# Retention and two MLPs on one core: free PSUM banks for two early steps, weight conversion one unit later, separate partial results for two stages

## The chip, the cores and the metric

The kernel runs on one core of a Trainium2 chip. The metric is the device time of one execution, in microseconds. Three runs of the kernel before are shown, with a median of 576.7 us (576.01 to 577.94).

## What is computed

Inputs are float32 q, k, v of shape 2 x 8 heads x 768 positions x 64, and a decay `lam` per head. The reference runs a chunked retention. For each head and each block of positions:

```python
intra = einsum('bhic,bhjc->bhij', qb, kb) * Dmask      # Dmask[i,j] = lam**(i-j), i >= j
intra = einsum('bhij,bhjd->bhid', intra, vb)
inter = einsum('bhid,bhde->bhie', qb * lam_pow, kv_state)
out   = intra + inter
kv_state = lam_block * kv_state + einsum('bhsd,bhse->bhde', kb * rev_pow, vb)
```

The result is reshaped to 1536 tokens x 512 and goes through two MLPs with float64 weights (512 x 2048 and 2048 x 512): `relu(x @ w_in)**2 @ w_out`, then `leaky_relu(x @ w_in, 0.01) @ w_out`.

## The kernel before, in words

**Retention** (function `retention`, lines 184 to 409) works on 12 units of 128 positions with all 8 heads: two batches of six. For a unit, SyncE (SP) loads k, q and v; TensorE transposes k and q (L294), ScalarE (ACT) copies the two transposes to SBUF (L298), VectorE (DVE) multiplies the transposed q by powers of `lam` straight out of PSUM (`scale_q`, L304); TensorE makes the scores (L311), DVE masks them with a table of powers (`mask`, L316), GpSimd (POOL) multiplies k by powers (L329), TensorE makes the state product (`state`, L335), DVE adds it to the state (L347, L349), and TensorE makes the output (`output`, L360 and L362), which ACT and DVE split into a high and a low part (L68, L69).

PSUM is one pool of eight banks (`bank()`, L58). A new bank is the one that has come free, so its first matmul waits for the last reader of what was in it. One bank, `idle`, is taken at the start for transposes that only keep TensorE at work (`warm`, L218).

The order on SP and TensorE is the order of the program text, written out by hand: for the first units in L368 to L390, then by the loop from L391, where pass i transposes unit i+2, loads units i+4 and i+2, makes state and output of unit i, masks unit i+1 and makes scores of unit i+2. On DVE, ACT and POOL the framework sets the order from its own reckoning of when operands are ready, except where `keep_in_program_order` puts an instruction behind the one traced before it on its engine.

**Weights** are float64 and are converted to float32 high and low parts on ACT and DVE from 1 MB raw tiles (`converting`, L98 to L144). A conversion is an ACT absolute value (L114) and seven DVE steps: L115, L116, L118, L121, L122, L125 and L137. `convert()` does the next step of what is at work. In the retention loop it is called once a pass for i = 3 to 9, with `pin=True`, which pins the DVE step that it yields and not the ACT operations. The raw tile itself is fetched in passes 1 and 9 (L398). In the MLPs `convert()` is called between groups of matmuls, without a pin.

**The first MLP** runs in four stages (l = 0, s = 0 to 3) of 512 hidden features. Stages 1 and 2 (`seven`) make the second product by seven multiplications instead of eight (`second_pair`, L617). Results go to DRAM tiles `spill`: `keep` (L607) copies a PSUM bank to one of nine SBUF buffers `f` (L61) and either stores it (SP) or adds it to what is there (an accumulating DMA issued by POOL, L613). Three products per pair, P1, P6 and P67, go to DRAM tiles `partial`: stage 1 stores them, stage 2 adds to them, and then ten DRAM-to-DRAM accumulating DMAs (L684) spread them over `spill`. In these two stages `activate_for_seven` (L479) holds eight of the nine `f` buffers in `later` until the sums of them are made.

Of the kernel before, what the change touches and what calls it, by code (L numbers as in the profile page):

```python
# [9 lines left out]
F32 = mybir.dt.float32  # L10
# [4 lines left out]
ALU = mybir.AluOpType  # L15
P = 128
# [3 lines left out]
def tile_retention_then_two_mlps(  # L20
# [12 lines left out]
    nc = tc.nc  # L33
    B, H, S, D = q.shape
# [4 lines left out]
    NP = H // 2  # L39
    TT = 512  # L40
# [9 lines left out]
    dram = ctx.enter_context(tc.tile_pool(name="dram", bufs=1, space=bass.MemoryType.DRAM))  # L50
# [7 lines left out]
    def bank():  # L58
        return psum.tile([P, 512], F32, tag="ps", name="ps")
# [113 lines left out]
    seven = {(0, 1), (0, 2)}  # L173
# [10 lines left out]
    def retention(ctx_att, att):  # L184
# [6 lines left out]
        tiny = ctx_att.enter_context(tc.tile_pool(name="tiny", bufs=1))  # L191

        units = [(b, c) for b in range(B) for c in range(NCH)]
        nats, qT, kT, qS, Pm, raw_scores = {}, {}, {}, {}, {}, {}

        def load(i, which="kqv"):
            b, c = units[i]
# [77 lines left out]
                DTr[:, par], bass.AP(tensor=row.tensor, offset=row.offset, ap=[[1, P], [2 * W, NP], [1, C]])))  # L275

        def column_of_powers():
            ps = bank()[:, 0:H]
            nc.tensor.transpose(ps, pw[:, 1:C + 1], ident[0:H, 0:H])
            nc.scalar.copy(kdec, ps)  # L280

# [6 lines left out]
        def transposes(i, names="kq"):  # L288
            for name in names:
                dst = {"k": kT, "q": qT}[name]  # L290
                ps = bank().rearrange("p (a s) -> p a s", a=NP)
                src = nats[i, name]
                for p in range(NP):
                    nc.tensor.transpose(ps[:, p, :], src[:, 2 * p:2 * p + 2, :].rearrange("s h d -> s (h d)"), ident)  # L294
                if i == 0:
                    warm(3 if name == "k" else 4)
                dst[i] = tr.tile([P, NP, C], F32, tag=name, name=name + "T", bufs=2)
                nc.scalar.copy(dst[i], ps)  # L298
            return ps

        def scale_q(i, ps):
            if units[i][1]:
                qS[i] = tr.tile([P, NP, C], F32, tag="qS", name="qS")
                ve.tensor_tensor(out=qS[i], in0=ps, in1=LR, op=ALU.mult)  # L304
# [8 lines left out]
        def mask(i):  # L313
            Pm[i] = wk.tile([P, 2, NP, C], F32, tag="Pm", name="Pm")
            for par in range(2):
                ve.tensor_tensor(out=Pm[i][:, par], in0=raw_scores[i][par], in1=DT[:, par], op=ALU.mult)  # L316
# [6 lines left out]
        def state(n):  # L323
            b, c = units[n]
            if c == NCH - 1:
                return
            kn, vn = nats[n, "k"], nats[n, "v"]
            kd = wk.tile([P, NP, 2, D], F32, tag="kd", name="kd")
            nc.gpsimd.tensor_tensor(  # L329
                out=kd, in0=kn.rearrange("s (a r) d -> s a r d", r=2),  # L330
                in1=kdec.rearrange("s (a r o) -> s a r o", r=2, o=1).to_broadcast([P, NP, 2, D]), op=ALU.mult)
            ps = bank()[:, 0:NP * D].rearrange("p (a e) -> p a e", a=NP)
            for p in range(NP):
                for par in range(2):
                    nc.tensor.matmul(ps[par * D:(par + 1) * D, p, :], kd[:, p, par, :], vn[:, 2 * p + par, :],  # L335
                                     start=True, stop=True)
            old, new = st[c % 2], st[(c + 1) % 2]
            if c:
                tmp = wk.tile([P, NP, D], F32, tag="tmp", name="tmp")
                for par in range(2):  # L340
                    r = slice(par * D, (par + 1) * D)
                    nc.gpsimd.tensor_tensor(out=tmp[r], in0=old[r, :, r],
                                            in1=LR[r, :, C - 1:C].to_broadcast([D, NP, D]), op=ALU.mult)
            for par in range(2):
                r = slice(par * D, (par + 1) * D)
                if c:
                    nc.vector.tensor_tensor(out=new[r, :, r], in0=ps[r], in1=tmp[r], op=ALU.add)  # L347
                else:
                    nc.vector.tensor_copy(new[r, :, r], ps[r])  # L349
# [32 lines left out]
        scale_q(1, q1)  # L382
        scores(1)
        state(0)
        mask(0)
        output(0)
        scale_q(2, transposes(2))
        state(1)
        mask(1)
        scores(2)  # L390
        for i in range(n_units):  # L391
            if i and i + 2 < n_units:
                scale_q(i + 2, transposes(i + 2))
            if i + 4 < n_units:
                load(i + 4, "kq")
            if i + 2 < n_units:
                load(i + 2, "v")
            if i in (1, 9):  # L398
                fetch()
            if i:  # L400
                if i > 1:
                    state(i)
                output(i)
                if i + 1 < n_units:
                    mask(i + 1)
                if i + 2 < n_units:
                    scores(i + 2)
            if 3 <= i <= 9:
                convert(pin=True)


# [190 lines left out]
            put(h, r22[h], r22[h], 1, 1)  # L602
            put(h, s2[h], s2[h], 0, 1)

    partial = [{n: dram.tile([P, TT], F32, name=f"partial{p}{n}") for n in ("P1", "P6", "P67")} for p in range(2)]

    def keep(src, dst, first):  # L607
        f = plain()
        nc.scalar.copy(f, src)  # L609
        if first:  # L610
            dma(dst, f)
        else:
            nc.gpsimd.dma_start(dst, f, accum_op=ALU.add)  # L613
# [1 line left out]


    def second_pair(s):  # L617
        begun = (0, s - 1) in seven
        (g0h, g0l), (g1h, g1l) = g[0], g[1]
        x = {  # L620
            "B11": [(g0h[:, 2 * h], g0l[:, 2 * h]) for h in range(2)],
            "B21": [(g0h[:, 2 * h + 1], g0l[:, 2 * h + 1]) for h in range(2)],
            "B22": [(g1h[:, 2 * h + 1], g1l[:, 2 * h + 1]) for h in range(2)],
            "T1": [(g1h[:, 2 * h], g1l[:, 2 * h]) for h in range(2)],
            "T2": [(tt[2][:, 0, h], tt[2][:, 1, h]) for h in range(2)],
        }
        ps = {}

        def product(p, where, a, b, start=True):
            if start:  # L630
                ps[p, where] = bank()
            ops = []
            for h in range(2):
                if a[0] == "A":
                    i, j = int(a[1]) - 1, int(a[2]) - 1
                    hi, lo = (w[:, j, (2 * p + i) * P:(2 * p + i + 1) * P] for w in wts[0, s, 1, h])
                else:
                    hi, lo = (sums[0, s, 1, h][:, part, int(a[1]) - 1, p] for part in range(2))
                bh, bl = x[b][h]
                ops += [(hi, bh), (hi, bl), (lo, bh)]  # L640
            three(ps[p, where], ops, start, True, not start)
            return ps[p, where]

        def kept(p, i, k):
            return spill[0][k][2 * p + i]

        def late_split(n, old, m):
            x[n] = x[old]
            with tc.high_priority(offset=400):
                for h in range(2):  # L650
                    split(*x[n][h], later[m(h)])

        both = range(2)
        for p in both:
            keep(product(p, "A", "A11", "B11"), partial[p]["P1"], not begun)
            yield True
        for p in both:
            keep(product(p, "C", "S1", "T1"), kept(p, 1, 1), False)
            yield True
        late_split("T3", "T1", lambda h: (1, 2 * h))  # L660
        for p in both:
            keep(product(p, "A", "A12", "B21", False), kept(p, 0, 0), False)
            yield True
        late_split("T4", "B21", lambda h: (0, 2 * h + 1))
        for p in both:
            keep(product(p, "C", "S4", "B22", False), kept(p, 0, 1), False)
            yield True
        for p in both:
            keep(product(p, "B", "S2", "T2"), partial[p]["P6"], not begun)
            yield True  # L670
        for p in both:
            keep(product(p, "D", "A22", "T4"), kept(p, 1, 0), False)
            yield True
        yield from first(0, s, 2)
        for p in both:
            keep(product(p, "B", "S3", "T3", False), partial[p]["P67"], not begun)
            yield True
        opened.add(("sums", 0, s + 1))
        if (0, s + 1) not in seven:
            for p in both:  # L680
                p1, p6, p67 = (partial[p][n] for n in ("P1", "P6", "P67"))
                for dst, src in ((p67, p1), (kept(p, 0, 1), p1), (kept(p, 0, 1), p6), (kept(p, 1, 0), p67),
                                 (kept(p, 1, 1), p67)):
                    nc.gpsimd.dma_start(dst, src, accum_op=ALU.add, max_dma_last_dim=TT)  # L684

    def second(l, s, t, ms=range(4)):
        last = s == NS - 1
# [94 lines left out]
```

## Time and profile before

| what | value |
|---|---|
| runs, median (lowest to highest) | 576.7 us (576.01 to 577.94) |
| the profiled execution's own time | 576.42 us |
| its span | 574.5 us |
| TensorE busy | 564.2 us, 98% |
| DVE busy | 418.4 us, 73% |
| ACT busy | 305.0 us, 53% |
| POOL busy | 83.9 us, 15% |
| granted TensorE clock | 1.0 of full speed in every slice |

The span lies inside the execution's own time, 1.92 us shorter. Busy shares are averages over stages with different limits, so a stage is read by the waits that end last there. L12 is line 12 of the kernel, and `ps` is any PSUM bank.

### The profile page before, as it was taken

How to read it: one execution, taken by the hardware profiler on the slowest of the kernel's cores; microseconds unless marked ns; L12 is line 12 of the kernel's file. 1: busy time of each engine (PE TensorE's matmuls, PEld its weight loads, DVE VectorE, ACT ScalarE, POOL GpSimd, SP SyncE). 2: the span in 40 equal slices, each digit the busy share in tenths (PEclk: the TensorE clock that was granted, in tenths of full speed). 3: DMA queues.
4: the chain of work that ended last, by engine and by line, in shares of the span. 5: the costliest groups of instructions: out<-in, count | busy, mean ns of one | idle time of the engine just before them, and what ended most of it. 6: DMA issues, size and time to landing. Idle time of an engine off the chain costs nothing.

```text
span 574.5 us, 8051 instructions
## 1 busy us (share of the span) xinstructions
PE 564.2 (98%) x3075; PEld 470.7 (82%) x3075; DVE 418.4 (73%) x589; ACT 305.0 (53%) x477; POOL 83.9 (15%) x101
## 2 busy tenths in 40 slices
PE   7989999999999999999999999999999999999997
PEld 6878888888788888888888888888888888888886
DVE  3879999999927599498478999929873996217222
ACT  2344598546757687758448374553562376225110
POOL 3426000000040105445000000000203011310000
PEclk9999999999999999999999999999999999999999
DMA  8997434665492649999713216341529523661432
GB/s 172 239 213 177 156 121 138 234 183 180 172 164 57 73 148 181 203 249 189 185 36 91 76 41 216 128 165 74 103 55 246 109 29 47 76 90 56 162 113 92
DMA packets 74071, 78.12 MB, mean 136 GB/s; under 512 B 40105, under 2 KB 46513, under 8 KB 74033
## 3 DMA queue, kind: packets, MB, share of 16 engines
q1 hardware_dynamic: 60448, 60.57, 34.6%
q0 software_dynamic: 13056, 16.78, 20.9%
q8 instruction: 24, 0.39, 0.3%
q10 hardware_dynamic: 528, 0.26, 0.2%
q14 instruction: 15, 0.11, 0.1%
HBM read 52.43 MB, written 27.80 MB: 140 GB/s over the span
## 4 chain that ended last, share of the span: by engine, by line
PE 74%; DVE 15%; DMA 6%; issue 3%; SPq 1%; ACT 1%; POOL 0%; DVEq 0%; POOLq 0%; ACTq 0%
PE ps L503 72%; DMA raw<-in_moe_w_in 2%; DVE rb L122 2%; DMA raw<-in_moe_w_out 2%; DVE hb L125 2%; DVE hb L118 2%; SPq L65 1%; DVE rb L121 1%; DVE hb L115 1%; DVE Pm L316 1%; DMA k<-in_k 1%; DVE xlo L69 1%; DVE w1l L137 0%; DVE g1l L474 0%; DVE sw L442 0%
## 5 line engine op out<-in xcount | busy, mean ns | idle before, releaser
L503 PE MATMUL ps<-xhi,w1h 128*128 128x512 f32 x288 | 112.1, 389 | 0.0
L503 PE MATMUL ps<-xlo,w1h 128*128 128x512 f32 x288 | 112.0, 389 | 0.0
L503 PE MATMUL ps<-xhi,w1l 128*128 128x512 f32 x288 | 112.0, 389 | 0.0
L613 POOL DMA_DIRECT2D spill<-f x48 | 46.9, 1047 | 347.6 <-ACT f L609 347.5
L609 ACT COPY f<-ps 128x512 f32<-128x512 f32 x84 | 48.9, 586 | 74.1 <-PE ps L503 72.7
L503 PEld LDWEIGHTS ps<-xhi,w1h 128*128 128x128 f32 x288 | 54.1, 188 | 11.3 <-issue 0.2
L503 PEld LDWEIGHTS ps<-xlo,w1h 128*128 128x128 f32 x288 | 54.1, 188 | 11.3
L503 PEld LDWEIGHTS ps<-xhi,w1l 128*128 128x128 f32 x288 | 54.1, 188 | 11.2
L474 DVE TENSOR_TENSOR g0l<-f,g0h 128x512 fp32r<-128x512 f32 x52 | 35.1, 687 | 33.7 <-ACT f L470 22.1
L503 PE MATMUL ps<-w2l,g0h 128*128 128x512 f32 (+1 forms) x132 | 50.5, 383 | 0.0
L503 PE MATMUL ps<-w2h,g0l 128*128 128x512 f32 (+1 forms) x132 | 50.5, 383 | 0.0
L503 PE MATMUL ps<-w2h,g0h 128*128 128x512 f32 (+1 forms) x132 | 50.5, 383 | 0.0
L137 DVE TENSOR_TENSOR w2l<-hb,w2h 128x1024 fp32r<-128x1024 f32 x16 | 19.5, 1222 | 39.8 <-ACT w2h L135 39.8
L114 ACT ACTIVATE hb<-raw 128x1024 f32<-128x1024 f32 x32 | 36.8, 1150 | 19.2 <-DVE w2l L137 7.4
L503 PE MATMUL ps<-g0h,w2h 128*128 128x512 f32 x104 | 40.5, 389 | 0.0
L503 PE MATMUL ps<-g0l,w2h 128*128 128x512 f32 x104 | 40.5, 389 | 0.0
L503 PE MATMUL ps<-g0h,w2l 128*128 128x512 f32 x104 | 40.5, 389 | 0.0
L122 DVE SCALAR_TENSOR_TENSOR rb<-raw,rb 128x1024 f32<-128x1024 uint32 x32 | 39.1, 1221 | 0.4
L125 DVE TENSOR_TENSOR hb<-hb,rb 128x1024 f32<-128x1024 f32 x32 | 39.1, 1220 | 0.4
L118 DVE SCALAR_TENSOR_TENSOR hb<-raw,hb 128x1024 uint32<-128x1024 uint32 x32 | 39.1, 1220 | 0.3
L567 DVE TENSOR_TENSOR f<-ps,f 128x512 f32<-128x512 f32 x40 | 26.2, 684 | 9.9 <-PE ps L503 9.9
L714 DVE TENSOR_TENSOR f<-ps,f 128x512 f32<-128x512 f32 (+1 forms) x25 | 16.7, 669 | 22.9 <-PE ps L503 21.7
(141 smaller groups left out, 1139.4 us busy)
## 6 DMA issues: line engine op xcount, KB each, us to landing
raw<-in_moe_w_in SPq DMA_DIRECT2D x16, 1024.0 KB, 5.6
raw<-in_moe_w_out SPq DMA_DIRECT2D x16, 1024.0 KB, 5.0
spill<-f POOLq DMA_DIRECT2D x48, 256.0 KB, 4.8
spill<-f SPq DMA_DIRECT2D x24, 256.0 KB, 2.6
f<-spill SPq DMA_DIRECT2D x24, 256.0 KB, 2.9
k<-in_k SPq DMA_DIRECT2D x12, 256.0 KB, 4.9
q<-in_q SPq DMA_DIRECT2D x12, 256.0 KB, 5.1
v<-in_v SPq DMA_DIRECT2D x12, 256.0 KB, 4.8
```

The lines of the kernel that those rows point to most:

```text
L65: return nc.sync.dma_start(dst, src)
L114: nc.scalar.activation(hf, w_hi.bitcast(F32), AF.Abs)
L118: yield ve.scalar_tensor_tensor(out=hb, in0=w_hi, scalar=0xC0000000, in1=hb, op0=ALU.bitwise_and, op1=ALU.bitwise_or)
L122: yield ve.scalar_tensor_tensor(out=rf, in0=w_lo, scalar=2.0 ** -52, in1=rf, op0=ALU.mult, op1=ALU.mult)
L125: yield ve.tensor_tensor(out=hf, in0=hf, in1=rf, op=ALU.add)
L137: yield ve.tensor_tensor(out=lo, in0=hf, in1=hi, op=ALU.subtract)
L474: nc.vector.tensor_tensor(out=glo, in0=r, in1=ghi, op=ALU.subtract)
L503: nc.tensor.matmul(ps, a, b, start=start and n == 0, stop=stop and n == len(ops) - 1, skip_group_check=again)
L567: ve.tensor_tensor(out=out, in0=ps[h, where], in1=other, op=ALU.add)
L609: nc.scalar.copy(f, src)
L613: nc.gpsimd.dma_start(dst, f, accum_op=ALU.add)
L714: nc.vector.tensor_tensor(out=a, in0=ps, in1=a, op=ALU.add)
```

## The change

In retention: the one column of powers goes into unused columns of the `idle` bank; the state product of unit 0 goes into the bank that held the k transposes of unit 1; the k transposes of unit 2 go into the bank that held the q transposes of unit 1, and are moved ahead of the mask and output of unit 0, with the q transposes left where they were; and the pinned conversion steps come in passes 4 to 10 instead of 3 to 9. In the first MLP: stages 1 and 2 each get partial tiles of their own, all stored by SP, and the ten DRAM-to-DRAM additions run after each of the two stages.

```diff
         def column_of_powers():
-            ps = bank()[:, 0:H]
+            ps = idle[:, P:P + H]
...
         def transposes(i, names="kq"):
...
-                ps = bank().rearrange("p (a s) -> p a s", a=NP)
+                whole = bank() if (i, name) != (2, "k") else read[1, "q"]
+                read[i, name] = whole
+                ps = whole.rearrange("p (a s) -> p a s", a=NP)
...
         def state(n):
...
-            ps = bank()[:, 0:NP * D].rearrange("p (a e) -> p a e", a=NP)
+            whole = bank() if n else read[1, "k"]
+            ps = whole[:, 0:NP * D].rearrange("p (a e) -> p a e", a=NP)
...
         state(0)
+        transposes(2, "k")
         mask(0)
         output(0)
-        scale_q(2, transposes(2))
+        scale_q(2, transposes(2, "q"))
...
-            if 3 <= i <= 9:
+            if 4 <= i <= 10:
                 convert(pin=True)
...
-    partial = [{n: dram.tile([P, TT], F32, name=f"partial{p}{n}") for n in ("P1", "P6", "P67")} for p in range(2)]
+    partials = {
+        s: [{n: dram.tile([P, TT], F32, name=f"partial{s}{p}{n}") for n in ("P1", "P6", "P67")} for p in range(2)]
+        for _, s in seven
+    }
...
     def second_pair(s):
-        begun = (0, s - 1) in seven
+        partial = partials[s]
...
-            keep(product(p, "A", "A11", "B11"), partial[p]["P1"], not begun)
+            keep(product(p, "A", "A11", "B11"), partial[p]["P1"], True)
...
         opened.add(("sums", 0, s + 1))
-        if (0, s + 1) not in seven:
-            for p in both:
+        for p in both:
...
```

P6 and P67 are changed in the same way as P1, and the five additions per pair under the last loop stay as they were.

## Rows read from the trace of the kernel before

**Rows 1.** Waits of TensorE over the span (us in total, times, longest).
```profile
PE ps L335 <- issue: 2.5, 1, 2.5
...
PE ps L503 <- DVE g1l L69: 0.5, 1, 0.5
```
**Rows 2.** The chain that ended last, 150 to 575 us (start, duration, what).
```profile
154.70 0.70 DVE g1l L69
...
155.44 415.72 PE ps L503 x1844
```
**Rows 3.** Busy time by stretch (length, PE, PEld, DVE, ACT, POOL, then clock and DMA).
```profile
42.57:62.04 19.47, 19.47 (x322) 17.34 (x320) 18.98 (x33) 8.97 (x15) 10.13 (x11) 1.00 0.84 223
62.04:155.40 93.36, 92.85 (x430) 76.72 (x430) 91.03 (x115) 64.85 (x96) 0.00 (x0) 1.00 0.47 158
```
**Rows 4.** Timeline of TensorE in retention (start, duration, line, [idle before <- releaser]).
```profile
14.06 0.69 PE L335 MATMUL ps<-v,kd 128*64 128x64 f32 x16 [2.52 <-issue]
14.54 1.15 PE L362 MATMUL ps<-Pm,v 128*64 128x128 f32 x16
15.63 0.66 PE L294 MATMUL ps<-ident,k 128*128 128x128 f32 x4
...
19.49 0.63 PE L294 MATMUL ps<-ident,q 128*128 128x128 f32 x4 [0.24 <-DMA q<-in_q]
...
32.73 1.16 PE L311 MATMUL ps<-qT,kT 64*128 64x128 f32 x16 [1.76 <-ACT qT L298]
...
34.85 0.69 PE L335 MATMUL ps<-v,kd 128*64 128x64 f32 x16
```
**Rows 5.** Timeline of DVE in retention.
```profile
13.27 1.29 DVE L316 TENSOR_TENSOR Pm<-ps,DTr 128x512 f32<-128x512 f32 x2 [6.79 <-DMA DTr<-tab]
14.47 0.68 DVE L304 TENSOR_TENSOR qS<-ps,LR 128x512 f32<-128x512 f32 x1
...
31.75 1.37 DVE L115 TENSOR_SCALAR hb<-hb 128x1024 f32<-128x1024 f32 x1 [2.71 <-ACT hb L114]
...
39.90 1.22 DVE L118 SCALAR_TENSOR_TENSOR hb<-raw,hb 128x1024 uint32<-128x1024 uint32 x1
...
42.57 1.28 DVE L316 TENSOR_TENSOR Pm<-ps,DTr 128x512 f32<-128x512 f32 x2
...
56.71 1.22 DVE L137 TENSOR_TENSOR w1l<-hb,w1h 128x1024 fp32r<-128x1024 f32 x1
...
62.04 0.69 DVE L115 TENSOR_SCALAR hb<-hb 128x1024 f32<-128x1024 f32 x1
```
**Rows 6.** Timeline of ACT, the first conversion and the third stage's first activation.
```profile
30.60 1.12 ACT L114 ACTIVATE hb<-raw 128x1024 f32<-128x1024 f32 x1 [3.47 <-DMA raw<-in_moe_w_in]
31.62 0.57 ACT L298 COPY kT<-ps 128x512 f32<-128x512 f32 x1
...
195.68 0.60 ACT L482 ACTIVATE f<-ps 128x512 f32<-128x512 f32 x1 [0.84 <-PE ps L503]
```
**Rows 7.** SP's issue of unit 4's v, and its time from issue to landing (us).
```profile
26.16 4.18 SPq L65 DMA_DIRECT2D v<-in_v  x1
...
v<-in_v SPq DMA_DIRECT2D x1, 256.0 KB, 7.9
```
**Rows 8.** Timeline of POOL: one k product, then accumulating DMAs of stage 2.
```profile
31.53 1.04 POOL L329 TENSOR_TENSOR kd<-k,kdec 128x512 f32<-128x512 f32 x1 [4.32 <-DMA k<-in_k]
...
217.47 0.86 POOL L613 DMA_DIRECT2D partial0P<-f  x1 [22.77 <-ACT f L609]
...
245.49 1.32 POOL L613 DMA_DIRECT2D partial0P<-f  x1
...
265.61 3.15 POOL L613 DMA_DIRECT2D spill<-f  x2
```
**Rows 9.** Costliest POOL groups: one of the four groups of L684 (busy us, mean ns).
```profile
L684 POOL DMA_DIRECT2D spill<-partial1P x4 | 5.5, 1610 | 1.2 <-DMA spill<-partial1P 1.2
```
**Rows 10.** Timeline of SP: the last partial store of stage 1.
```profile
183.02 0.32 SPq L65 DMA_DIRECT2D partial1P<-f  x1
```

More of the change, by code (lines that the diff above doesn't have):

```diff
@@ L193, in retention @@
         units = [(b, c) for b in range(B) for c in range(NCH)]
-        nats, qT, kT, qS, Pm, raw_scores = {}, {}, {}, {}, {}, {}
+        nats, qT, kT, qS, Pm, raw_scores, read = {}, {}, {}, {}, {}, {}, {}
         def load(i, which="kqv"):
@@ L668, in second_pair @@
         for p in both:
-            keep(product(p, "B", "S2", "T2"), partial[p]["P6"], not begun)
+            keep(product(p, "B", "S2", "T2"), partial[p]["P6"], True)
             yield True
@@ L675, in second_pair @@
         for p in both:
-            keep(product(p, "B", "S3", "T3", False), partial[p]["P67"], not begun)
+            keep(product(p, "B", "S3", "T3", False), partial[p]["P67"], True)
             yield True
         opened.add(("sums", 0, s + 1))
-        if (0, s + 1) not in seven:
-            for p in both:
[L681 to L684, printed above, removed]
+        for p in both:
+            p1, p6, p67 = (partial[p][n] for n in ("P1", "P6", "P67"))
+            for dst, src in ((p67, p1), (kept(p, 0, 1), p1), (kept(p, 0, 1), p6), (kept(p, 1, 0), p67),
+                             (kept(p, 1, 1), p67)):
+                nc.gpsimd.dma_start(dst, src, accum_op=ALU.add, max_dma_last_dim=TT)
     def second(l, s, t, ms=range(4)):
```

## Prediction

> **What bounds the kernel now.** I read the waits of TensorE first. It is busy for 564.2 of the span's 574.5 us, so a change of order alone can win back at most its idle time, about 10 us, and the start and the end of the program hold part of that. Of the waits inside, three matter here: 2.52 us before the first state product, 1.76 us before unit 5's scores, and 0.53 us in stage 1 of the first MLP, for DVE's low part of g1 [rows 1, 2, 4].
>
> Then the chain that ended last, because idle time on the busiest engine need not be the bound. From 155.44 us on it is one piece of TensorE work, 415.72 us [rows 2]. What released that piece is DVE, which finished g1's low part at 155.40. Before that DVE has hardly a pause: 91.03 us busy of the 93.36 between 62.04 and 155.40, and 18.98 of the 19.47 between 42.57 and 62.04 [rows 3]. So up to 155 us there are two clocks. TensorE reaches the product that needs g1 at about 154.9 and waits 0.53 us for DVE. Whatever TensorE gains before that point is lost there again unless DVE also finishes g1 sooner; and each microsecond by which DVE falls back goes into the end in full. The question to put to each edit is what it does to DVE's queue.
>
> **The change part by part.**
>
> *Bank for the first state product, column of powers in the idle bank.* The state product of unit 0 waits 2.52 us and starts at 14.06, just after the first half of unit 0's mask (the two halves take 1.29 us from 13.27) [rows 4, 5]: its bank was one that this mask had to read. In another bank it can start some 2 us sooner. But the output of unit 0 needs the mask itself, which ends at 14.56 and waits for the table of powers from DRAM (DVE idle 6.79 us, released by that DMA) [rows 5]. The output starts at 14.54 already, right behind it [rows 4]. So this wait costs nothing now beyond what the mask costs, and its removal gives 0. Upper bound: the 0.48 us from 14.06 to 14.54, if the state product were the only work ahead of the output.
>
> *Unit 2's k transposes ahead of unit 0's output.* They need the bank that unit 1's q transposes were in, which unit 1's `scale_q` reads on DVE: 14.47 to 15.15, behind the mask [rows 5]. If DVE keeps this order, the four transposes (0.66 us [rows 4]) cannot start before 15.15, and the output queued behind them on TensorE moves from 14.54 to about 15.8, 1.26 us later. The transposes no longer follow it, so from there on TensorE is about 1.26 - 0.66 = 0.6 us late. If DVE takes `scale_q` first, it is up to 0.66 us early. Neither lasts: at 19.49 TensorE waits for unit 3's q to land anyway (0.24 idle) [rows 4], and what is left of the lateness, some 0.4 us, goes into the 1.76 us before 32.73. I put this part at 0, with -0.7 and +0.4 as ends should those covers go.
>
> *Conversion one pass later.* The ACT absolute value waits 3.47 us for the raw tile, which lands at about 30.6; behind it on ACT stand the copies of unit 5's transposes, and TensorE's wait of 1.76 us is for the second of them [rows 4, 6]. On DVE step L115 is queued in front of unit 3's state sums and waits 2.71 us [rows 5]. With the pass moved, L115 leaves that place. The absolute value is a different matter: it is not pinned. In the trace it already stands ahead of unit 5's k copy [rows 6], which comes earlier in the program text of the same pass; it was placed by when its operand was reckoned to land, not by the text. The fetch of the raw tile is not moved, so I expect it in the same place on ACT, with TensorE's 1.76 us unchanged.
>
> DVE's side is then a count. At 42.57 (the mask of unit 7) DVE is about level with what TensorE and ACT hand it, before and after. From there to 62.04, where the second conversion begins, DVE did four steps of the first (L121, L122, L125, L137). One pass later it has five left, L118 being the extra one, at 1.22 us [rows 5]. It can hide in DVE's idle time of this stretch, 19.47 - 18.98 = 0.49 us [rows 3], wholly or not at all: DVE reaches 62.04's work 0.73 to 1.22 us later. I take the middle, 1.0. Of the 2.33 us idle up to 155.40 nearly all follows DVE's own steps through ACT or a raw buffer, so I let none of it absorb anything. The last step, L137, then falls next to unit 10's state sums. If it goes first, TensorE's last output waits up to 1.2 us, but that is the same microsecond, not a second one: the later of the two clocks counts.
>
> [...] L115 took 1.37 us at 31.75, beside a POOL product of k that ran from 31.53 to 32.57; the same step took 0.69 at 62.04, where POOL had nothing to do [rows 5, 8]. That loss of 0.68 lies ahead of 42.57, so it is not in my sum. [...]
>
> *Partial results per stage.* Six additions leave POOL's queue in stage 2 and become SP stores (0.32 us of issue [rows 10]); ten DRAM-to-DRAM additions of up to 1.61 us each [rows 9], at most 16 us, join POOL's queue after about 183 us. POOL has room: 22.77 us idle before stage 2's first product [rows 8]. Nobody reads those sums before stage 2's own additions to the same tiles, and TensorE has no wait at all after 155.44 [rows 2]. Cost 0; without that cover, see the third rival.
>
> **Sum.** 0 + 0 + 1.0 + 0 on the profiled execution's 576.42 us: 577.4 us. That execution lies 0.3 below the median shown, 576.7, which I don't add. I count 0.3%, 1.7 us, as what a measurement of this kernel can tell from no change, so this is no change.
>
> **The rivals.**
>
> *1. The absolute value does move behind unit 5's copies.* Then TensorE's 1.76 us goes. What is late next is unit 4's v: issued at 26.16, landed 7.9 us later, 34.06 [rows 7], needed by the state product that started at 34.85 [rows 4]. The transfers ahead of it are the same, so TensorE gains only 34.85 - 34.06 = 0.8 us. DVE gets its input 0.8 earlier too, and still has the extra step: +1.0 - 0.8 = +0.2, 576.6 us. For it speaks that the text moves by a pass; against it, that the operation is placed by its operand. Chance 0.22.
>
> *2. Faster.* The 1.76 us goes in full, v being no limit (its issue held SP for 4.18 us [rows 7], so its landing hangs on traffic), and DVE's order near 154.7 happens to put g1 sooner, so that the 0.53 goes as well: 576.42 - 1.76 - 0.53 = 574.1 us. Both are needed, since with DVE as it is the gain would be swallowed at 155. Chance 0.13.
>
> *3. Slower, through the `f` buffers.* The last four results of stage 1 sit in `f` until POOL has issued and landed their additions. If POOL's order puts these behind the ten new ones, which hang on each other, they are late: in stage 2 POOL went from the P67 partial at 245.49 to 268.76, 23.3 us, for the same chain [rows 8]. From 183.3 that ends at 206.6, and a landing of a few microseconds (7.9 at most in [rows 7]) makes 214.5. Stage 2's activations take an `f` each from 195.68 on [rows 6]; one group is twelve matmuls, 415.72 / 1844 x 12 = 2.7 us [rows 2], and with four held of nine the sixth is due at 195.68 + 5 x 2.7 = 209.2. It decides from there: ACT would stand up to 5.3 us, and PSUM would cover part. [...] Against it: POOL's waits in stage 2 stopped nothing. Chance 0.16.
>
> **How the numbers follow.** My forecast, DVE one step later and nothing else, has 0.45; the rivals 0.22, 0.13 and 0.16; 0.04 stays for other orders that the framework may find. Faster by over 0.3%: rival 2 and a little of the rest, 0.15. Slower by over 0.3%: rival 3 and the upper edge of the forecast with the lock, 0.18. Within: 0.67. The range goes from 574.8, short of rival 2, to 579.2, which holds the forecast with a lock and most of rival 3.
>
> **What would show it.** Right: the wait before the first state product gone and the output of unit 0 no earlier; ACT's absolute value still ahead of unit 5's k copy, TensorE's 1.76 us unchanged; the second conversion beginning on DVE about 1 us after 62.04; the wait on g1's low part grown from 0.53 to about 1.5 us; no TensorE wait in stage 2. Wrong: that wait gone or smaller, a TensorE wait after 185 us, or a chain that leaves DVE before 155 us.

## The result and the profile after

The changed kernel takes 580.4 us (median of six executions, 578.06 to 581.39) against 576.4 us for the kernel before beside it (575.83 to 577.94): 1.006 times, interval 1.0041 to 1.0079. It is slower, by more than the 0.3% that the prediction counts as no change, and above the range of the prediction (574.8 to 579.2).

The profiled execution took 581.12 us. That is 4.70 us over the profiled one of before (576.42), and the chain that ended last splits it. The piece of TensorE work without a pause that began at 155.44 [rows 2] now begins at 158.53, 3.09 us later, and is 417.33 us long instead of 415.72, 1.61 us more; 3.09 + 1.61 = 4.70. The waits of TensorE and that chain (start, duration, what), after:

```profile
PE ps L296 <- DVE qS L306: 2.2, 1, 2.2
...
PE ps L313 <- ACT qT L300: 1.5, 2, 1.2
PE ps L507 <- DVE g1l L69: 1.3, 1, 1.3
PE ps L507 <- ACT g1h L68: 1.3, 1, 1.3
```
```profile
157.87 0.61 DVE g1l L69
158.49 0.04 issue
158.53 417.33 PE ps L507 x1844
```

The 0.53 us for the low part of g1 [rows 1] has become two waits at the same product, 1.30 us for its high part (ScalarE, behind the sum that DVE makes at L495) and 1.31 us for its low part. The product before which they stand is the only one at which TensorE waits after retention, and DVE is behind both.

**Front.** TensorE, start of each step with the idle time before it, after:

```profile
11.71 0.69 PE L338 MATMUL ps<-v,kd 128*64 128x64 f32 x16
14.56 0.66 PE L296 MATMUL ps<-ident,k 128*128 128x128 f32 x4 [2.16 <-DVE qS L306]
15.14 1.09 PE L365 MATMUL ps<-Pm,v 128*64 128x128 f32 x16
...
19.61 0.63 PE L296 MATMUL ps<-ident,q 128*128 128x128 f32 x4 [0.31 <-DMA q<-in_q]
...
32.31 1.16 PE L313 MATMUL ps<-qT,kT 64*128 64x128 f32 x16 [1.22 <-ACT qT L300]
```

The first state product starts at 11.71 instead of 14.06 [rows 4], without a wait. The 2.16 us before unit 2's k transposes have taken its place, and the output of unit 0 goes 0.60 us later, at 15.14. By unit 3's q transposes 0.12 is left of that, because they wait for their DMA in both kernels (0.24 us before [rows 4], 0.31 after). At 32.31 TensorE is 0.42 us earlier than before.

**DVE in retention.** The steps of the first conversion, and POOL's products of k beside them, after:

```profile
47.78 1.17 DVE L121 TENSOR_SCALAR rb<-hb 128x1024 uint32<-128x1024 uint32 x1
52.17 1.79 DVE L122 SCALAR_TENSOR_TENSOR rb<-raw,rb 128x1024 f32<-128x1024 uint32 x1
57.19 1.22 DVE L125 TENSOR_TENSOR hb<-hb,rb 128x1024 f32<-128x1024 f32 x1
62.70 1.23 DVE L137 TENSOR_TENSOR w1l<-hb,w1h 128x1024 fp32r<-128x1024 f32 x1
63.84 0.69 DVE L115 TENSOR_SCALAR hb<-hb 128x1024 f32<-128x1024 f32 x1
```
```profile
43.70 1.76 POOL L331 TENSOR_TENSOR kd<-k,kdec 128x512 f32<-128x512 f32 x1 [7.39 <-PE ps L338]
...
47.36 1.04 POOL L331 TENSOR_TENSOR kd<-k,kdec 128x512 f32<-128x512 f32 x1 [0.49 <-POOL tmp L345]
...
51.84 1.05 POOL L331 TENSOR_TENSOR kd<-k,kdec 128x512 f32<-128x512 f32 x1 [0.57 <-POOL tmp L345]
```

The same two steps in the kernel before, with POOL's product beside L122:

```profile
43.77 0.69 DVE L121 TENSOR_SCALAR rb<-hb 128x1024 uint32<-128x1024 uint32 x1
47.67 1.22 DVE L122 SCALAR_TENSOR_TENSOR rb<-raw,rb 128x1024 f32<-128x1024 uint32 x1
```
```profile
47.78 2.00 POOL L329 TENSOR_TENSOR kd<-k,kdec 128x512 f32<-128x512 f32 x1 [1.02 <-issue]
```

Read the starts against each other. Before, L122 started 0.11 us ahead of POOL and took 1.22, as it does where POOL has no product (L122 at 67.64), and POOL took 2.00 for a product that took 1.04 at 24.89. After, POOL started 0.42 and 0.33 us ahead of L121 and L122, and these took 1.17 and 1.79 instead of 0.69 and 1.22: 0.48 + 0.57 = 1.05 us on DVE. The second conversion begins 1.80 us late, at 63.84. In these meetings the operation that started second took longer than elsewhere, in both directions. It was not held to the other's end: POOL ended 0.62 and 0.72 us behind the two DVE starts, and DVE lost 0.48 and 0.57. Where the recorded texts speak of a lock, they mean such a step held up by a POOL product. The prediction's range has room for one of up to 1.04 us, the length of a product; that was the author's estimate, and why the two engines slow each other no run shows. Here there were two such meetings, and 1.05 is measured.

**DVE in the MLP, and TensorE's clock.** Windows (length; PE, PEld, DVE, ACT, POOL busy; granted clock; DMA), after:

```profile
42.15:63.84 21.69, 21.20 (x342) 18.64 (x342) 21.20 (x35) 9.27 (x15) 8.79 (x11) 1.00 0.77 204
63.84:157.79 93.95, 92.07 (x414) 75.59 (x410) 87.80 (x111) 62.81 (x93) 0.00 (x0) 1.00 0.44 146
155.00:160.00 5.00, 2.38 (x8) 1.38 (x7) 4.96 (x7) 3.83 (x7) 0.00 (x0) 0.95 0.25 33
160.00:165.00 5.00, 5.00 (x17) 4.01 (x16) 4.97 (x11) 3.45 (x6) 2.32 (x3) 0.71 0.95 313
```

In 160 to 165 us TensorE makes 17 matmuls at a granted clock of 0.71; the kernel before makes 24 there, at 1.00:

```profile
160.00:165.00 5.00, 5.00 (x24) 4.14 (x23) 1.44 (x3) 3.44 (x7) 4.37 (x5) 1.00 0.92 124
```

That is the 1.61 us. From the second conversion to the start of the low part, DVE takes 93.95 us after and 154.70 - 62.04 = 92.66 before [rows 2, 3], so it loses another 1.29. That is not more work: it is busy for 87.80 us of the stretch, against 91.03 - 0.69 = 90.34 before without the low part itself. It is idle for 6.15 us (2.3 before), 2.56 of them at one place, where ACT's L114 waits for a raw tile (DVE's timeline, then ACT's):

```profile
121.25 0.69 DVE L115 TENSOR_SCALAR hb<-hb 128x1024 f32<-128x1024 f32 x1 [2.56 <-ACT hb L114]
...
155.32 0.69 DVE L495 TENSOR_TENSOR f<-f 128x512 f32<-128x512 f32 x1
155.93 0.69 DVE L121 TENSOR_SCALAR rb<-hb 128x1024 uint32<-128x1024 uint32 x1
156.65 1.23 DVE L122 SCALAR_TENSOR_TENSOR rb<-raw,rb 128x1024 f32<-128x1024 uint32 x1
157.79 0.69 DVE L69 TENSOR_TENSOR g1l<-f,g1h 128x512 fp32r<-128x512 f32 x1
```
```profile
120.09 1.12 ACT L114 ACTIVATE hb<-raw 128x1024 f32<-128x1024 f32 x1 [4.34 <-DMA raw<-in_moe_w_out]
```

The fetch of that tile was issued at 111.94, 8.15 us before L114 could start; the like fetch of the kernel before, issued at 110.11, took 4.91. Between the sum L495 and the low part there stand two conversion steps now; in the kernel before there stood four short weight sums. So DVE runs in another order, and it meets a tile that has not landed.

### The profile page after: what moved, and what is told of

Its sections match the earlier page's. It is cut to its first block, busy times and chain, and to the rows that moved or that the text cites. A ratio compares the mean times of both kernels' runs of the same rounds, so it can differ in the third digit from the quotient of the medians.

```text
span 579.4 us, 8054 instructions
## 1 busy us (share of the span) xinstructions
PE 567.2 (98%) x3075; PEld 472.3 (82%) x3075; DVE 418.6 (72%) x589; ACT 304.6 (53%) x477; POOL 88.2 (15%) x105
## 4 chain that ended last, share of the span: by engine, by line
PE 86%; DVE 7%; DMA 3%; SPq 1%; ACT 1%; issue 1%; ACTq 0%
PE ps L507 84%; SPq L65 1%; DMA raw<-in_moe_w_in 1%; DMA q<-in_q 1%; DVE Pm L318 1%; DVE rb L122 1%; DVE hb L125 1%; PE ps L363 1%; DVE hb L118 1%; PE ps L296 0%; PE ps L365 0%; DVE xlo L69 0%; DVE rb L121 0%; PE ps L313 0%; DVE st L350 0%
## 5 line engine op out<-in xcount | busy, mean ns | idle before, releaser
L114 ACT ACTIVATE hb<-raw 128x1024 f32<-128x1024 f32 x32 | 36.8, 1150 | 20.0 <-DVE w2l L137 5.7
L122 DVE SCALAR_TENSOR_TENSOR rb<-raw,rb 128x1024 f32<-128x1024 uint32 x32 | 39.7, 1239 | 0.4
```

The lines of the kernel that those rows point to most:

```text
L114: nc.scalar.activation(hf, w_hi.bitcast(F32), AF.Abs)
L122: yield ve.scalar_tensor_tensor(out=rf, in0=w_lo, scalar=2.0 ** -52, in1=rf, op0=ALU.mult, op1=ALU.mult)
```

## The experiments

**Which edit.** Only the passes of the conversion are changed in the first, everything but them in the second.

```diff
 conv_only: the kernel before, with
-            if 3 <= i <= 9:
+            if 4 <= i <= 10:
 no_conv: the changed kernel, with
-            if 4 <= i <= 10:
+            if 3 <= i <= 9:
```

> The kernel before with the conversion steps in passes 4 to 10 and nothing else changed. Theory 1 (the moved conversion makes DVE late for g1's low part, TensorE waits, and its clock falls behind the wait): 579 to 581 us, the second conversion's L115 on DVE near 63.8 instead of 62.04, the waits of TensorE between 150 and 160 us together 2 us or more instead of 0.53. Rival A (the bank edits cost it) and rival B (the extra DRAM-to-DRAM additions cost it): 576 to 577 us.

> The changed kernel with the conversion steps back in passes 3 to 9: bank edits and separate partials alone. Theory 1: 576 to 577 us, one wait of about 0.5 us near 155. Rivals A and B: 578.5 us or more, with the lost time in retention (A) or behind 174 us (B). It should also show the 2.2 us wait of unit 2's k transposes on DVE's scale_q, with nothing of it left at unit 3's q.

conv_only: 581.4 us, 1.009 (1.0059 to 1.0122). no_conv: 576.2 us, 0.9999 (0.9983 to 1.0015). The whole loss is in the line of the passes; the bank edits and the partial results are worth nothing that can be measured. conv_only is slightly above its expected 579 to 581. In no_conv the k transposes of unit 2 wait 2.63 us, and TensorE waits for the low part of g1 0.61 us in stage 1 and 0.38 at the like product of stage 2. In conv_only's profiled execution (579.45 us, the shortest of its four) L121 and L122 took 1.17 and 1.79 again, the second conversion began at 64.10, and the two waits were 1.14 and 1.31 us. The clock stayed at 1.00:

```profile
155.00:160.00 5.00, 2.55 (x10) 1.59 (x9) 4.97 (x7) 3.83 (x7) 0.00 (x0) 1.00 0.19 27
160.00:165.00 5.00, 5.00 (x23) 4.14 (x23) 4.97 (x11) 3.80 (x8) 2.27 (x3) 1.00 0.99 316
```

The product starts at 158.56, 3.12 late, and the piece behind it is 415.71 us, that of before. So nearly the same waits end with the clock fallen or not, and the 1.6 us is not part of every execution.

**The steps beside POOL.** In the changed kernel the products of k go to ScalarE from unit 8 on, and DVE's order stays as it was.

```diff
+            if n > 7:
+                ...
+                        nc.scalar.activation(kd[:, p, par, :], kn[:, h, :], AF.Copy, scale=kdec[:, h:h + 1])
+            else:
               nc.gpsimd.tensor_tensor(
```

> The changed kernel with the k products of units 8 to 10 made by eight ACT operations each instead of one POOL operation; DVE's order stays as in the changed kernel. [...] Rival C (DVE's new order and the later raw tiles alone set the end, the lock costs nothing): 580 to 581, unchanged.

If the two longer steps are what the end pays for, 579.4 us was expected, or 578 with the clock up. It took 578.2 us, 1.0038 (1.0019 to 1.0057). With no product on POOL beside them the two steps take 0.68 and 1.22 us, and the second conversion begins at 63.07, 1.03 us after 62.04: the prediction's 1.0. The waits are still 0.85 and 1.31 us and the product starts at 157.26, 1.82 late. So with neither step held up the extra step becomes 1.82 us at g1 in this execution. The clock stayed at 1.00 and the piece behind is 415.75 us. Against 580.4 of the changed kernel this puts the two longer steps and what follows from them at about 2 us of the median (1.3 by the two ratios), and the two intervals overlap, so the size is rough.

**Does DVE's lateness pass to the end?** In the kernel before, four operations of 0.6 us stand ahead of the low part of g1.

```diff
+                if m == 2 and not padded:
+                    padded.append(True)
+                    for _ in range(4):
+                        nc.vector.tensor_tensor(out=glo[:, m], in0=r, in1=r, op=ALU.subtract)
```

> The kernel before with four DVE operations of about 0.6 us added ahead of g1's low part in stage 1; two short sums of weights move behind it, so DVE is some 2.2 us later there. Theory 1: the wait of 0.53 grows to about 2.7, and the end by 2.2 us at least, 578.6; if the granted clock also falls in the 5 us behind the wait, by up to 1.6 us more, 580.2. Rival D (TensorE has room to catch up behind 155 us, or the wait is hidden): 576.4 to 577 us.

580.0 us, 1.0072 (1.0051 to 1.0094). The wait for the low part is 2.53 us, and the clock falls as in the changed kernel (the window, and the last piece of the chain):

```profile
160.00:165.00 5.00, 5.00 (x17) 3.97 (x16) 3.50 (x7) 3.42 (x6) 1.90 (x2) 0.66 0.56 58
```
```profile
159.27 417.31 PE ps L508 x1844
```

So lateness at this product does pass on. It doesn't measure the price cleanly: L122 took 2.06 us there (at 47.84) and not 1.22, in an order that is the kernel before's up to the product. That POOL's product of k started first this time is an estimate from the 1.79 us of L122 in the changed kernel.

**The absolute value.** It is pinned to its pass, so that it goes behind unit 5's copies: in the changed kernel, and in that one with the old passes.

```diff
-        nc.scalar.activation(hf, w_hi.bitcast(F32), AF.Abs)
+        absolute = nc.scalar.activation(hf, w_hi.bitcast(F32), AF.Abs)
+        if not begun_mlp:
+            tc.keep_in_program_order(absolute)
```

> The changed kernel with the ACT absolute value of retention's conversion pinned behind the ACT operation traced before it, so that it leaves its place ahead of unit 5's copies. Rival 1 of the prediction, tried on purpose: TensorE's wait of 1.22 us before unit 5's scores goes; if unit 4's v is late next, the state product of unit 4 waits for it until about 34.1 and starts 0.4 us sooner than in the changed kernel. Theory 1: DVE sets the end, so the gain is 0.4 us at most, 580 us (or 577.7 to 578.5 where the clock stays up); if TensorE's place in retention set the end, 1.2 us or more lower than the changed kernel in like runs.

> Bank edits and partials without the moved conversion, and the absolute value pinned as above. TensorE's wait before unit 5's scores (0.2 to 1.8 us) goes, DVE's wait of 2.7 us for the absolute value moves. Theory 1: DVE reaches the second conversion up to 0.8 us sooner, the end comes 0 to 0.8 us below the kernel before, ratio 0.9986 to 1.0. If the landing of unit 4's v binds: no gain.

581.0 us, 1.0073 (1.0053 to 1.0092), and 576.2 us, 0.9999 (0.999 to 1.0008). The wait before unit 5's scores is 0.2 us in both, and neither is faster; the first is above its expected range. In the first, unit 4's v is late next, as rival 1 had it:

```profile
34.76 0.69 PE L340 MATMUL ps<-v,kd 128*64 128x64 f32 x16 [1.25 <-DMA v<-in_v]
```

The profiled execution of the first (578.77 us, the shortest of its four) shows something more. The second conversion begins at 64.17, later than in the changed kernel, and from there to g1's low part DVE does the same 110 operations in the same order. But it waits only 0.19 us for L114 on the way, not 2.83, and the product at g1 starts only 0.79 us late. The lateness comes back 64 us on: in stage 2 TensorE waits 0.38 and 0.58 us, behind a raw tile that took 8.41 us, and the chain ends 2.31 us later than before (DVE's timeline, then the chain):

```profile
127.69 0.69 DVE L117 TENSOR_SCALAR hb<-hb 128x1024 f32<-128x1024 f32 x1 [0.19 <-ACT hb L114]
```
```profile
156.23 42.92 PE ps L509 x188
201.10 8.41 DMA raw<-in_moe_w_in
...
220.32 353.15 PE ps L509 x1568
```

**The way to g1's low part.** One high part of g1 is rounded on DVE instead of ScalarE, in the changed kernel; and, with the old passes and the pin, as the best that the runs so far pointed to (best: no_conv with both edits).

```diff
+                if m == 2:
+                    nc.vector.tensor_copy(ghi[:, m], later[0, m])
+                    nc.vector.tensor_tensor(out=glo[:, m], in0=later[0, m], in1=ghi[:, m], op=ALU.subtract)
+                else:
```

> The changed kernel with the high part of the disputed quarter of g1 (m = 2) rounded on DVE instead of ACT, so that DVE goes on to the low part without a round trip, in which two conversion steps of 1.74 us stood. Theory 1 (TensorE waits for DVE's order at this one place): the low part ends 0.8 to 1.5 us sooner, the two waits of 1.3 us shrink to about 1.3 together, the end comes 1 us sooner, or 2.5 if the clock then stays up: 578 to 579.4. Rival E (DVE's backlog as a whole sets the end, wherever the low part stands): 580 to 581.

> As the last one, and the high part of the disputed quarter of g1 rounded on DVE. Theory 1: the wait of 0.53 near 155 goes as well: 0.5 to 1.3 us below the kernel before, ratio 0.9977 to 0.9991; nothing if another wait takes its place.

582.4 us, 1.0093 (1.0064 to 1.0121), and 577.0 us, 1.0021 (1.0 to 1.0042). Neither gains time. In the first the waits became 1.70 and 1.24 us, since L122 came between the two new steps, and the granted clock went lower, to 0.52 in 160 to 165. In best the wait in stage 1 is gone, as expected, and another takes its place: 0.72 us for the low part at the like product of stage 2 (218.27), so the wait has moved by 64 us. Shortening one hand-over gained nothing here, where DVE had no time to spare at the next.

**The clock.** Twelve spare matmuls stand in front of the product in the changed kernel, where TensorE would wait.

```diff
+        if s == 1:
+            spare = bank()
+            for _ in range(12):
+                nc.tensor.matmul(spare, wts[0, s, 1, 0][0][:, 0, 0:P], x["B11"][0][0], start=True, stop=True)
```

> The changed kernel with twelve spare 128x512 matmuls (0.23 us each, 2.7 us, result unused) on TensorE in stage 1, ahead of the product that needs g1's low part. The twelve stand where TensorE would wait anyway (1.30 + 1.31 us), so by themselves they cost about 0 to 0.3 us. Theory (the fall of the granted clock follows from TensorE standing still there): the wait on g1's low part is 0 to 0.5 us, the clock of 160 to 165 us stays at 1.0, the piece behind the product is 415.7 us and not 417.3, and the time is 578.5 to 579.5. Rival (the clock falls for another reason, or its fall is no cost): 0.5 to 0.8 in 160 to 165 us again, and 580 to 581.5 us.

581.7 us, 1.0101 (1.007 to 1.0133): half a hit. The wait is gone and the clock stays at 1.00 through 155 to 175 us, but the time doesn't follow. TensorE now reaches the like product of stage 2 before DVE, whose chain goes back to a raw tile that took 8.46 us to land (203.64 to 212.10):

```profile
221.83 0.50 PE L507 MATMUL ps<-g1h,sw 128*128 128x512 f32 x1 [0.45 <-ACT g1h L68]
...
222.91 0.50 PE L507 MATMUL ps<-g1l,sw 128*128 128x512 f32 x1 [0.59 <-DVE g1l L69]
```

In the changed kernel that wait isn't there: TensorE arrives later, and the tile had landed by 211.19. So the clock's 1.6 us is real in the trace and yet was not won here: DVE and its raw tiles limit a second time, 64 us on, as in after_pinabs and best.

**One step too many, by itself.** The kernel before with one more pinned DVE operation (two SBUF inputs, 1.23 us) in pass 10.

```diff
+            if i == 10:
+                spent = cv.tile([P, 2, NP, C], U32, tag="rb", name="rb")
+                tc.keep_in_program_order(ve.tensor_tensor(out=spent.bitcast(F32), in0=DTr, in1=DTr, op=ALU.add))
```

> The kernel before with one more pinned VectorE operation in the retention loop (two SBUF inputs, 128x1024, result unused), so that the count of steps is off by one with passes 3 to 9 unchanged. Theory of the count (one step late at the second conversion passes one for one into the end, and a two-input step can be held by a GpSimd product besides): the second conversion begins 1.0 to 2.3 us after 62.04, the wait on g1's low part is about 1.5 to 3.0 us, 577.3 to 579.5 us. Rival (what made the changed kernel late is the other order of VectorE's work in the MLP, and the extra step is absorbed): second conversion 0 to 0.5 us late, wait of about 0.5 us, 576.2 us.

578.0 us, 1.003 (1.0011 to 1.0048), in the theory's range of times. In the profiled execution (581.43 us, among the longest of twelve) no conversion step behind 42 us took longer than 0.69 or 1.22 us, and the second conversion began at 62.68, only 0.64 late, less than the theory's 1.0. Still the product started at 157.81, 2.37 late, with waits of 1.41 and 1.32 us and the same order on DVE as in the changed kernel, and a wait for a raw tile on the way (DVE's timeline, then the chain):

```profile
129.27 0.70 DVE L115 TENSOR_SCALAR hb<-hb 128x1024 f32<-128x1024 f32 x1 [3.02 <-ACT hb L114]
```
```profile
157.81 418.46 PE ps L506 x1844
```

So a step that is left over costs time with no change of the passes at all: 1.7 us of the median, between 0.6 and 2.8 by the interval. That it costs more than its own 1.23 us shows in this long execution, which lost 3.02 us to the raw tile and 2.74 us in the piece behind the product (418.46 us), where the granted clock was 0.69 and 0.63 in 155 to 165 us; the median alone does not show it.

**The count restored.** The changed kernel, the first step still a pass later, but two steps in pass 4; without and with the pin of the absolute value.

```diff
-            if 4 <= i <= 10:
+            if 4 <= i <= 9:
                 convert(pin=True)
+            if i == 4:
+                convert(pin=True)
```

> The changed kernel with the count of steps restored: one pinned conversion step in each of passes 4 to 9, and a second one in pass 4, so that seven steps are done by pass 9 as before; the first still begins a pass later. VectorE's order from unit 7's mask on is that of the kernel before. Theory (the loss is the step that is left over, and all else follows from it): the second conversion begins at 62.0 +- 0.5, the wait on g1's low part is about 0.5 us and from VectorE alone, the clock of 155 to 165 us stays at 1.0, 576.0 to 576.6 us. Rival (the later start in itself costs, by the lock or by the state sums): second conversion 0.5 us or more late, 577 us or more.

> The same with ScalarE's absolute value of the first conversion pinned, so that it no longer stands ahead of unit 5's copies. Theory (TensorE's wait before unit 5's scores gives way to unit 4's v, and whatever TensorE gains before 155 us is lost at g1's low part): wait on unit 5's scores under 0.3 us, wait on g1's low part 0.4 to 1.0 us, 575.8 to 576.5 us. Rival (the 1.2 us wait before unit 5's scores was on the path): 575.2 us or less.

576.9 us, 1.0009 (0.9997 to 1.0021), and 577.6 us, 1.0019 (1.0008 to 1.003). The first is the kernel before again: steps of 0.68 and 1.22 us, the second conversion at 61.73, four weight sums ahead of g1's low part, a wait for that part of 0.8 us, and the product where it was (the chain, then a window):

```profile
155.42 415.71 PE ps L509 x1844
```
```profile
160.00:165.00 5.00, 5.00 (x24) 4.14 (x23) 1.41 (x3) 3.40 (x7) 4.35 (x5) 1.00 0.93 136
```

This settles which part of the edit costs the time: with the later start kept and only the left-over step taken back, the loss is gone to within 0.6 us (the median is 0.3 above the expected range). With the pin the time misses its range, 575.8 to 576.5: TensorE is ahead at unit 5's scores and in the end 0.7 us worse by the median; why was not followed up. No version beat the kernel before.

## Why the prediction was wrong, step by step

- **Bank for the first state product; unit 2's transposes: right.** 0 was predicted and no_conv measured 0.9999. The output of unit 0 was 0.60 us late, not 1.26, because `scale_q` ended about 0.6 us earlier than in the profile of before (14.50 and 15.15); the DMA of unit 3's q absorbed it, as predicted.
- **Absolute value on ScalarE: the place right.** It stays ahead of unit 5's copies (30.14 to 31.30, the k copy at 31.20). TensorE's wait is 1.22 us and not the unchanged 1.76; the raw tile let L114 start 0.46 us sooner. after_pinabs shows rival 1's mechanism, v binding next, and that it wins nothing.
- **Partial results: right.** The ten additions run on POOL from 174.02 on, and TensorE has no wait behind 158.53. Rival 3, which came nearest to the time (576.42 + 2.6 + 1.0 = 580.0, with about half of its 5.3 us on TensorE), did so by luck: TensorE has none of the waits in stage 2 that it rests on.
- **"DVE reaches 62.04's work 0.73 to 1.22 us later. I take the middle, 1.0": the mechanism right, the size short by 0.8.** It came 1.80 later: about 1.2 for the extra step, 1.05 for the two steps beside POOL's products, and 0.42 back, since DVE reached unit 7's mask at 42.15 instead of 42.57. The 0.49 us of idle time hid nothing (it is 21.69 - 21.20 = 0.49 after, too). Without it, 1.80 - 1.05 = 0.75 in this trace and 1.03 in after_kdact, both inside the step's range. The row that could have said so was in the trace of before: POOL's product beside L122 took 2.00 us and not 1.04, so the two already met, with DVE ahead by 0.11 us. Moved by a pass, L121 and L122 met it with POOL ahead by 0.42 and 0.33. The lock of up to 1.04 us in the prediction's range no run shows; what the runs showed in its place is 0.48 and 0.57 us more (after), and nothing in after_kdact, where these products are not on POOL.
- **The pass-through from 62.04 to 155: this is the step that failed.** The prediction let the microsecond pass one for one ("I let none of it absorb anything") and had no term for a raw tile that has not landed. In six of the traces with a step left over DVE does the same 110 operations in the same order from the second conversion to g1's low part, so they can be compared (us; late against the kernel before, 62.04 and 154.70):

| run | second conversion late | DVE's waits for L114 on the way | low part of g1 late |
|---|---|---|---|
| changed kernel | 1.80 | 2.83 | 3.09 |
| conv_only | 2.06 | 2.52 | 3.12 |
| after_fill | 2.51 | 2.05 | 3.16 |
| after_kdact | 1.03 | 1.84 | 1.82 |
| before_late | 0.64 | 3.02 | 2.37 |
| after_pinabs | 2.13 | 0.19 | 0.80 |

  Each row is one profiled execution. Ahead of the longest of these waits in the changed kernel, conv_only, after_kdact and before_late L114 itself waits for a raw tile, by 2.40 to 4.34 us; the kernel before waits 0.56 us for L114 on the way. Where DVE meets such a tile before it has landed, the lateness grows, by 0.65 to 1.73 us; where it does not, it shrinks by 1.33. The new order by itself is no loss in these traces, since it puts some 2.5 us less DVE work ahead of the low part; the waits are what made 1.80 into 3.09. Why a tile lands late in some executions and not in others no run shows.
- **TensorE's clock: no term.** The prediction saw 1.0 in every slice and priced the wait at its length. In the profiled execution the clock fell behind the wait, 1.61 us more. It is not in every execution: two of the six have a mean clock of 1.000 over the whole span, one of 578.06 us and the longest, 581.39. A mean below that does not say where the clock fell: no_conv's 0.997 goes with 1.00 in each window from 140 to 170 us and with slow matmuls at 15.46, where the 16 of unit 0's output take 1.79 us, and 1.09 in the changed kernel. How much of the median's 4.0 us is the clock stays open.
- **The sum.** Of the profiled execution's 4.70 us the prediction had 1.0. The later start of the second conversion adds 0.80, the way to g1 1.29, and the clock 1.61.

## What to carry to other kernels

Count the pinned steps that a shifted loop leaves over, and not where they begin: here the step too many was the whole loss, and restoring the count with the later start kept took it back. Where the busiest helper engine hands over to the bottleneck with no time to spare, do not carry a lateness through one for one: compare the order of its operations first, then look for the transfers that it will meet before they land. Here those waits, up to 3.02 us, decided whether the lateness grew or shrank. A POOL product that took 2.00 us beside L122, and 1.04 elsewhere, was the sign here that the two meet; before a step is moved, look for who would start first in the new place.

## What the runs showed of the hardware

- Where a DVE conversion step and a POOL product of k met, the one that started second took longer than elsewhere: with L122 0.11 us ahead, it took 1.22 us and POOL 2.00 (the kernel before); with L122 0.33 behind, it took 1.79 and POOL 1.05 (after); with L121 0.42 behind, it took 1.17 and not 0.69, and POOL 1.04 (after).
- TensorE's granted clock fell to 0.71 in 160 to 165 us behind two waits of 1.30 and 1.31 us with one matmul between them (after). Matmuls of 128x512 then stand 0.43 us apart (160.87 to 161.30), until about 162.6; in the kernel before, at 1.00, they stand 0.23 apart (160.34 to 160.57). In conv_only the clock stayed at 1.00 in 155 to 165 us behind waits of 1.14 and 1.31. What decides between the two no run shows.
- A like fetch of a raw tile took 8.15 us from issue to the start of L114 in the changed kernel (111.94 to 120.09) and 4.91 in the kernel before (110.11 to 115.02).
